# Three SBUF rings of an attention stage one buffer deeper, and a new set of planner ranks

## The chip, the cores and the metric

The kernel runs on one core of one Trainium2 chip. The metric is the device time of one execution in microseconds, and lower is better. Of the kernel before three timed runs are given, and one more execution that was taken with the profiler; all rows below come from that one.

## The reference, cut to what matters

Three stages, all in float32: linear attention with an exponential feature map, then two feed-forward layers, each on 2304 tokens of width 512 with a hidden width of 2048.

```python
def phi(x):                                   # q, k: (4, 8, 576, 64), w_phi: (64, 128)
    proj = np.einsum('bhsd,df->bhsf', x, w_phi)
    proj = proj - np.max(np.abs(proj), axis=-1, keepdims=True)
    return np.concatenate([np.exp(proj), np.exp(-proj)], axis=-1)
q_p, k_p = (phi(q), phi(k))
kv = np.einsum('bhsf,bhsd->bhfd', k_p, v);  z = np.sum(k_p, axis=2)
num = np.einsum('bhsf,bhfd->bhsd', q_p, kv)
den = np.einsum('bhsf,bhf->bhs', q_p, z)[..., None] + 1e-06
...
h = x @ w_in;   g = np.where(h > 0.0, h, np.exp(np.minimum(h, 0.0)) - 1.0);  x = g @ w_out
h = x @ w2_in;  g = h * np.clip(h + 3.0, 0.0, 6.0) / 6.0;                   out = g @ w2_out
```

## The kernel before, in words

**A planner writes the order.** Nearly every piece of work is a `Step` with an engine, an estimated duration, the steps that it comes after, the ring tokens that it takes and uses, and a rank. `in_order` plays the engines forward in time on those estimates. At each turn it takes, on each engine, the steps that could start within 0.3 us (`WINDOW`) of the soonest one and picks the one of lowest rank. The instructions of each engine are then issued in the order that comes out. On the chip an engine works through that order strictly and waits where an operand is late. A ring of n buffers is a limit in the planner and, through the tile's `bufs`, in the kernel: the (n+1)th writer waits for the last reader of the first buffer.

**Attention** is done in 8 units u, each two heads of two batches, 576 rows each. The sequence is cut into nine row blocks; a tile has a name such as k01: side k, blocks 0 to 3 ("0") or 4 to 7 ("1"), head 0 or 1; x8 is the ninth block of both sides. For each tile the steps are:

- PJ (PE, L439): projection of raw k or q by w_phi into PSUM; 18 blocks times two heads in a unit, and each float32 product is recorded as two instructions. It uses 64 rows of the array. In units 1 to 7 the steps are PJk0 (all k tiles), PJx8 and PJq0 (all q tiles).
- MX and SB (DVE, L449, L463): peak of the absolute value, then projection minus peak, written to SBUF tile `shk` (ring KB), `shq` (ring QB) or `sh`.
- EX (ACT, L472): the two exponentials of a k tile, `shk` to `kp` (ring KPB). KV (PE, L501, 128 rows): accumulation of kv and z from `kp` and v. ST (ACT, L510): kv to SBUF.
- QT (PE, L515, 64 rows): transposition of `shq`. QE (ACT, L532): exponentials of q, into `e`.
- NM (PE, L554, 128 rows): numerators and denominators, three steps in a unit. RT (DVE, L562, L563): reciprocal of the denominator, tile `dn`. RB (DVE, L567): the quotient, tile `nr` (ring NRB). XT (PE, L515): its transposition. XC (ACT, L583): copy to the x tile of the feed-forward layer.

The rank of such a step is `u * PERIOD` minus the length of the work that hangs on it, plus `BIAS`, looked up by name and unit (`KVk10@0`), by name (`KVk10`), or by kind (`KV`).

**The layers** have their PE order written out by hand (the list `order`); 8 groups g per layer. A group has seven products P1 to P7 for each of two block pairs (L841, one level of Strassen's scheme; in the first pair P6, P5 and P3 add to the bank that P1 opened, with a copy by ACT, `snap` L863, in between), two products H for the fifth block (L855), and products O (L908) that add to the output, which DVE adds up in x (`sums`, L924). The weights arrive as 64-bit floats and are made into pairs of float32 parts by ACT, DVE (L772, L778) and POOL (L766, L782, L788, L799, L808). Activation results are split by ACT (L886) and DVE (`gate_lo`, L889). The operands X of a layer are sums and differences of the blocks of x (`x_add`, L818, steps a...), split into a high part (L824, steps h...) and a low part (`x_lo`, L827, steps l...). The list `ON_POOL` says which of the a... and l... steps run on POOL instead of DVE: a10S40 is layer 1 (of 0, 1), block pair 0, operand S4, half 0. `SHIFT` adds to the rank of a single step.

Of the kernel before, what the change touches and what calls it, by code (L numbers as in the profile page):

```python
# [23 lines left out]
KB, QB, KPB, EB, NRB, MXB, WB, GB = 3, 6, 3, 4, 2, 6, 3, 2  # L24
PERIOD, PROJ, TURN = 21.5, 0.228, 0.13
BIAS = {
# [1281 lines left out]
```

## Time and profile before

| | before |
|---|---|
| median of three runs | 891.4 us (891.36 to 891.97) |
| profiled execution | 891.67 us |
| its span, first to last instruction | 889.8 us |
| PE busy | 879.9 us, 99% |
| DVE, ACT, POOL busy | 647.7, 567.3, 415.4 us |
| granted TensorE clock, mean | 1.000 |

The profiled execution takes 1.9 us more than its span and lies 0.27 us above the median. Busy shares are means over stages with different limits. The attention stage runs to about 150 us, the first layer to about 500 us, the second to the end. PE's busy time is no measure of how densely it works, since its instructions overlap and their ends are modelled; the distance from start to start tells more.

### The profile page before, as it was taken

To read this page: it belongs to the slowest core of one execution; us is meant where nothing else is said; L and a number is where in the kernel's file an instruction comes from. 1 tells how busy PE (TensorE), PEld (TensorE's weight loads), DVE (VectorE), ACT (ScalarE), POOL (GpSimd) and SP (SyncE) were. 2 spreads that over 40 slices of the span, in tenths; PEclk is the share of its full clock that TensorE was granted. 3 is DMA by queue.
4 is the path that set the end of the run, shared out by engine and by line. 5 is a ranking of instruction groups with operands and counts; after the bars stand their busy time and mean duration, and the time that the engine had idled before them with its cause. 6 is when DMAs were issued, how large, how long until landed. Compare 5 with 4: busy or idle time off the path is not lost.

```text
span 889.8 us, 18053 instructions
## 1 busy us (share of the span) xinstructions
PE 879.9 (99%) x7018; PEld 753.1 (85%) x7018; DVE 647.7 (73%) x1190; ACT 567.3 (64%) x1215; POOL 415.4 (47%) x584
## 2 busy tenths in 40 slices
PE   8999999999999999999999999999999999999998
PEld 7999997888888888888888788888888888888887
DVE  6999987647676767776777997576767676767656
ACT  6887889877575756565667777755545454545331
POOL 0268517745444444444444866565535354444200
PEclk9999999999999999999999999999999999999999
DMA  8545310011111111101111001112111111110013
GB/s 253 147 141 134 110 51 14 13 60 47 48 49 48 48 44 40 60 34 51 36 48 56 17 13 60 48 36 82 49 60 37 48 48 48 48 48 25 1 71 143
DMA packets 42678, 53.66 MB, mean 60 GB/s; under 512 B 21344, under 2 KB 21728, under 8 KB 42592
## 3 DMA queue, kind: packets, MB, share of 16 engines
q1 hardware_dynamic: 42448, 52.44, 18.8%
q8 instruction: 55, 0.90, 0.4%
q14 instruction: 31, 0.25, 0.1%
q10 hardware_dynamic: 144, 0.07, 0.0%
HBM read 47.78 MB, written 4.72 MB: 59 GB/s over the span
## 4 chain that ended last, share of the span: by engine, by line
PE 94%; DVE 5%; issue 0%; ACT 0%; DVEq 0%
PE ps_y L908 44%; PE ps_h L841 34%; PE ps_h L855 5%; PE ps_a L501 3%; PE ps_p L439 3%; PE ps_n L554 3%; PE ps_t L515 2%; DVE mx L449 1%; DVE shk L463 1%; DVE shq L463 1%; DVE nr L567 1%; PE ps_w L349 0%; DVE x L924 0%; DVE dn L563 0%; DVE dn L562 0%
## 5 line engine op out<-in xcount | busy, mean ns | idle before, releaser
L924 DVE TENSOR_TENSOR x<-ps_y,x 128x512 f32<-128x512 f32 (+1 forms) x267 | 174.9, 659 | 86.3 <-PE ps_y L908 82.9
L841 PE MATMUL ps_h<-x_S,w_in 128*128 128x512 f32 x768 | 190.2, 390 | 1.4 <-ACT mb L863 1.4
L841 PEld LDWEIGHTS ps_h<-x_S,w_in 128*128 128x128 f32 x768 | 143.7, 188 | 31.9 <-ACT mb L863 2.2
L841 PE MATMUL ps_h<-x_A,w_in 128*128 128x512 f32 x576 | 143.6, 390 | 0.0
L799 POOL TENSOR_TENSOR w_in<-w_bi,w_in 128x256 fp32r<-128x256 f32 x128 | 95.8, 766 | 70.4 <-ACT w_in L795 70.0
L841 PEld LDWEIGHTS ps_h<-x_A,w_in 128*128 128x128 f32 x576 | 107.2, 188 | 21.7
L908 PE MATMUL ps_y<-gb,w_out 128*128 128x512 f32 (+1 forms) x576 | 119.1, 354 | 0.8 <-DVE gb L889 0.5
L908 PE MATMUL ps_y<-w_out,gb 128*128 128x512 f32 (+1 forms) x486 | 117.5, 386 | 0.0
L908 PEld LDWEIGHTS ps_y<-gb,w_out 128*128 128x128 f32 x576 | 96.8, 189 | 17.5 <-DVE gb L889 1.0
L908 PEld LDWEIGHTS ps_y<-w_out,gb 128*128 128x128 f32 x486 | 90.6, 188 | 18.5
L766 POOL TENSOR_SCALAR w_a<-w_a 128x256 f32<-128x256 f32 x128 | 53.9, 422 | 98.3 <-ACT w_a L761 96.3
L782 POOL TENSOR_TENSOR w_bi<-w_bi,w_a 128x256 int32<-128x256 int32 x64 | 48.4, 758 | 108.7 <-DVE w_a L778 108.7
L908 PE MATMUL ps_y<-ga,w_out 128*128 128x512 f32 x384 | 92.6, 390 | 0.0
L908 PE MATMUL ps_y<-w_out,ga 128*128 128x512 f32 x384 | 92.3, 390 | 0.0
L908 PEld LDWEIGHTS ps_y<-w_out,ga 128*128 128x128 f32 x384 | 71.2, 188 | 14.2
L908 PEld LDWEIGHTS ps_y<-ga,w_out 128*128 128x128 f32 x384 | 71.2, 188 | 14.1
L782 POOL TENSOR_TENSOR w_bo<-w_bo,w_a 128x256 int32<-128x256 int32 x64 | 49.3, 772 | 65.3 <-DVE w_a L778 65.3
L882 DVE SCALAR_TENSOR_TENSOR ps_h<-ma,ps_h 128x512 f32<-128x512 f32 x80 | 55.4, 694 | 30.8 <-ACT ma L878 17.6
L863 ACT COPY mb<-ps_h 128x512 f32<-128x512 f32 x64 | 37.7, 589 | 58.0 <-PE ps_h L841 57.9
L808 POOL TENSOR_TENSOR w_out<-w_bo,w_out 128x256 fp32r<-128x256 f32 x64 | 47.3, 739 | 55.0 <-ACT w_out L804 54.5
L868 DVE TENSOR_TENSOR ps_h<-ps_h,mb 128x512 f32<-128x512 f32 x64 | 44.5, 696 | 35.9 <-ACT w_a L761 21.4
L889 DVE TENSOR_TENSOR gb<-ps_h,gb 128x512 fp32r<-128x512 f32 x80 | 54.5, 684 | 10.7 <-ACT gb L886 10.5
(80 smaller groups left out, 1455.8 us busy)
## 6 DMA issues: line engine op xcount, KB each, us to landing
w<-in_moe_w_in_dram SPq DMA_DIRECT2D x64, 256.0 KB, 2.6
w<-in_moe_w_out_dram SPq DMA_DIRECT2D x64, 256.0 KB, 2.6
vb<-in_v_dram SPq DMA_DIRECT2D x16, 288.0 KB, 4.9
out_dram<-x SPq DMA_DIRECT2D x17, 256.0 KB, 2.0
raw_k<-in_k_dram SPq DMA_DIRECT2D x7, 576.0 KB, 4.8
raw_q<-in_q_dram SPq DMA_DIRECT2D x7, 576.0 KB, 4.0
raw_k<-in_k_dram SPq DMA_DIRECT2D x1, 320.0 KB, 4.3
raw_q<-in_q_dram SPq DMA_DIRECT2D x1, 320.0 KB, 4.6
```

The lines of the kernel that those rows point to most:

```text
L766: nc.gpsimd.tensor_scalar(out=st["a"], in0=st["a"], scalar1=W_MOST, scalar2=W_LEAST, op0=ALU.min, op1=ALU.max)
L782: nc.gpsimd.tensor_tensor(out=b_, in0=b_, in1=st["a"].bitcast(I32), op=ALU.add)
L799: nc.gpsimd.tensor_tensor(out=t[:, 1], in0=F[key], in1=t[:, 0].bitcast(F32), op=ALU.subtract)
L808: nc.gpsimd.tensor_tensor(out=t[:, 1], in0=F.pop((m, w, 1, c)), in1=t[:, 0].bitcast(F32), op=ALU.subtract)
L841: nc.tensor.matmul(out=PS[ps_], lhsT=t[:, a_, kk], rhs=X[pr, op][x_][kk], start=(opens and i == 0), stop=(i == 5), skip_group_check=True,)
L855: nc.tensor.matmul(out=PS[ps_][:, 256 * fi:256 * fi + 256], lhsT=t[:, a_, kk], rhs=XB["x"][x_][2 * half + kk], start=(i == 0), stop=(i == ...
L863: nc.scalar.copy(out=MAIN[key], in_=PS[ps_])
L868: V.tensor_tensor(out=PS[to], in0=PS[ps_], in1=MAIN[key], op=ALU.add)
L882: V.scalar_tensor_tensor(out=PS[ps_], in0=MAIN[key], scalar=s, in1=PS[ps_], op0=o0, op1=o1)
L889: V.tensor_tensor(out=GG[key][:, 1], in0=PS.pop(ps_), in1=GG[key][:, 0].bitcast(F32), op=ALU.subtract)
L908: nc.tensor.matmul(out=o, lhsT=a_, rhs=b_, start=(fi + j == 0), stop=(fi == 1 and j == 2),)
L924: V.tensor_tensor(out=part, in0=ps, in1=part, op=ALU.add)
```

## The change

Three ring sizes rise by one: KB (the k tiles after the subtraction, `shk`) 3 to 4, KPB (their exponentials, `kp`) 3 to 4, NRB (the quotients, `nr`) 2 to 3. All of `BIAS`, most of `SHIFT`, and the list `ON_POOL` (34 names to 24: 18 taken out, 8 put in) are replaced. No instruction is added or removed; the order within each engine changes, and some of the a... and l... steps change engine.

```diff
 PB, TB = 6, 6
-KB, QB, KPB, EB, NRB, MXB, WB, GB = 3, 6, 3, 4, 2, 6, 3, 2
+KB, QB, KPB, EB, NRB, MXB, WB, GB = 4, 6, 4, 4, 3, 6, 3, 2
 PERIOD, PROJ, TURN = 21.5, 0.228, 0.13
 BIAS = {
-    "EX": -1284.5, "EXk00": -1287.9, "EXk00@0": -1229.4, "EXk00@7": -1290.5, "EXk01": -1250.5,
...
-    "EXx80@7": -1242.9, "KV": 1569.7, "KVk00": 688.3, "KVk00@0": 682.5, "KVk00@7": 808.9,
-    "KVk01": 633.4, "KVk01@0": 645.8, "KVk01@7": 620.8, "KVk10": 1610.3, "KVk10@7": 1634.4,
-    "KVk11": 1597.7, "KVk11@0": 1563.8, "KVx80": 1557.8, "KVx80@0": 1532.5, "KVx81": 1583.7,
-    "KVx81@0": 1549.4, "KVx81@7": 1541.4, "MX": -3939.8, "MXk00@7": -3937.8, "MXk01": -4172.3,
...
-    "MXx80@7": -3946.6, "MXx81": -4129.4, "MXx81@0": -4119.1, "MXx81@7": -4091.7, "NM": -92.1,
-    "NM0": -74.9, "NM1@7": -90.8, "NM2@0": -105.6, "NM2@7": -636.7, "PJ": 1001.6, "PJk0": 758.9,
-    "PJk0@0": 794.6, "PJk0@7": 747.3, "PJk1": 975.9, "PJk1@0": 520.4, "PJq0": 947.9,
-    "PJq0@0": 909.3, "PJq0@7": 856.1, "PJq1": 927.0, "PJq1@0": 399.3, "PJx8": 751.8,
...
+    "EX": 25.3, "EXk00": 26.5, "EXk00@7": 27.2, "EXk01": 78.0, "EXk01@0": 73.1, "EXk10": 49.5,
...
+    "EXx80": 59.2, "EXx80@7": 37.3, "KV": 378.3, "KVk00": 385.8, "KVk00@0": 349.3, "KVk00@7": 405.1,
+    "KVk01": 502.1, "KVk01@0": 510.3, "KVk01@7": 503.0, "KVk10": 675.9, "KVk10@0": 1437.7,
+    "KVk10@7": 687.0, "KVk11": 385.7, "KVk11@7": 461.5, "KVx80": 423.0, "KVx80@0": 418.8,
+    "KVx80@7": 312.8, "KVx81": 399.1, "KVx81@0": 456.9, "KVx81@7": 356.4, "MX": -6882.6,
...
+    "MXx81@7": -6951.9, "NM": -1437.3, "NM0": -1632.4, "NM0@7": -1579.5, "NM1@0": -1579.8,
+    "NM1@7": -1576.6, "NM2": -1468.9, "NM2@0": -1511.6, "NM2@7": -1471.5, "PJ": 4015.9,
+    "PJk0": 4028.6, "PJk0@0": 4003.2, "PJk0@7": 4039.1, "PJk1": 3924.7, "PJk1@0": 1417.4,
+    "PJq0": 4043.7, "PJq0@0": 4053.6, "PJq1": 3951.8, "PJq1@0": 1361.5, "PJx8": 3983.4,
...
 ON_POOL = """
-a01S11 a01S21 a01S31 a01S40 a10S10 a10S11 a11S11 a11S20 l00S40 l00S41 l01A121 l01A221 l01S10
-l01S11 l01S21 l01S30 l01S31 l01S40 l01S41 l04x1 l04x2 l04x3 l10A220 l10A221 l10S10 l10S11 l10S40
-l11A110 l11A121 l11A220 l11S30 l11S31 l11S41 l14x3
+a01S10 a01S11 a01S31 a10S10 a10S40 a11S10 a11S11 a11S31 l00S40 l00S41 l01A221 l01S11 l01S30
+l01S31 l04x2 l04x3 l10A220 l10A221 l10S11 l10S30 l10S31 l11A221 l14x1 l14x3
 """.split()
```

## Rows read from the trace of the kernel before

**Rows 1.** Page, part 1: engine, busy us, share, instructions.

```profile
PE 879.9 (99%) x7018; PEld 753.1 (85%) x7018; DVE 647.7 (73%) x1190; ACT 567.3 (64%) x1215; POOL 415.4 (47%) x584
```

**Rows 2.** Chain that ended last, whole run: start us, us, what, instructions.

```profile
53.75 4.61 PE ps_n L554 x144
...
240.88 5.44 PE ps_h L841 x24
...
287.52 5.44 PE ps_h L841 x24
```

**Rows 3.** The same chain, one unit of attention.

```profile
103.37 4.58 PE ps_n L554 x144
107.95 0.69 PE ps_t L515 x12
108.64 1.84 PE ps_p L439 x32
110.48 0.18 PE ps_t L515 x6
110.66 2.02 PE ps_a L501 x64
112.68 0.96 PE ps_t L515 x20
113.64 2.64 PE ps_a L501 x96
```

**Rows 4.** Groups of PE instructions over the run: KV and NM, with counts.

```profile
L501 PE MATMUL ps_a<-vb,kp 128*64 128x65 f32 (+1 forms) x1280 | 40.0, 224 | 1.3 <-ACT kp L472 0.7 <-issue 0.5
L554 PE MATMUL ps_n<-st,e 128*64 128x65 f32 x1152 | 36.7, 222 | 0.0
```

**Rows 5.** Busy time by window: start:end, length, PE, PEld, DVE, ACT, POOL, clock.

```profile
53.75:70.30 16.55, 16.34 (x438) 15.45 (x438) 15.71 (x34) 14.91 (x39) 11.84 (x15) 1.00 0.54 150
...
132.81:153.06 20.25, 18.90 (x229) 15.63 (x230) 13.82 (x26) 18.42 (x39) 13.49 (x13) 1.00 0.05 16
...
497.00:515.00 18.00, 17.23 (x88) 14.13 (x87) 17.25 (x28) 13.40 (x29) 16.01 (x16) 1.00 0.00 0
```

**Rows 6.** Timeline, the unit of rows 3: start, us, engine, what, [idle before].

```profile
105.24 2.19 ACT L472 ACTIVATE kp<-shk 128x512 f32<-128x512 f32 x4 [0.69 <-DVE shk L463]
...
107.49 0.68 DVE L463 TENSOR_TENSOR shk<-ps_p,mx 128x512 f32<-128x512 f32 x1
...
108.27 0.19 DVE L563 RECIPROCAL dn<-dn 128x6 f32<-128x6 f32 x1
...
108.57 0.56 DVE L567 TENSOR_TENSOR nr<-ps_n,dn 128x384 f32<-128x384 f32 x1
...
111.84 1.15 ACT L472 ACTIVATE kp<-shk 128x512 f32<-128x512 f32 x2 [0.61 <-ACT x L583]
...
113.56 2.07 ACT L532 ACTIVATE e<-ps_t 128x512 f32<-128x512 f32 x4 [0.56 <-PE ps_t L515]
```

**Rows 7.** Timeline of the first unit: PE's KV and QT with waits.

```profile
12.58 0.34 PE L501 MATMUL ps_a<-vb,kp 128*64 128x65 f32 x4 [0.49 <-ACT kp L472]
...
14.73 0.97 PE L515 MATMUL ps_t<-ident,shq 64*128 64x64 f32 x16 [0.60 <-DVE shq L463]
```

**Rows 8.** Chain at the start of the first layer: ACT's copies, then products H.

```profile
144.18 0.60 ACT mb L863
...
146.51 0.59 ACT mb L863
...
150.19 2.87 PE ps_h L855 x24
```

**Rows 9.** Timeline between the two layers: DVE, and PE waiting for it.

```profile
503.29 1.12 DVE L818 TENSOR_TENSOR x<-x 128x512 f32<-128x512 f32 x1
...
506.86 5.27 PE L908 MATMUL ps_y<-gb,w_out 128*128 128x512 f32 x22 [0.53 <-DVE gb L889]
...
509.34 0.67 DVE L818 TENSOR_TENSOR x<-x 128x512 f32<-128x512 f32 x1
```

152 rows, old and new, of tables (BIAS, SHIFT) are left out of this document.

## The prediction

> **What bounds the kernel now.** I read the page's busy line first: PE is busy for 99% of the span, DVE for 73% [rows 1]. No stretch shows PE at less than full clock, 2.4 GHz [rows 5]. A busy PE is not a dense PE, so the second view is the chain that ended last, where start-to-start distances count. In the first layer a group begins at 240.88 and the next at 287.52, 46.64 us later [rows 2]. A group holds 84 products P and 96 products O of 512 columns, 5.44 / 24 = 0.2267 us each [rows 2], 40.80 us, and 48 products of 256 columns (24 H, 24 O of the fifth block) at 2.87 / 24 = 0.1196 us [rows 8], 5.74 us. That is 46.54 of 46.64 us. So the layers are PE's own time, 16 such groups, some 740 us in which a rank can move nothing that counts. What can move is the attention stage, its two ends, and the passage between the layers.
>
> Third, one unit of attention. NM begins at 53.75 in one unit and at 103.37 three units later, a period of 16.54 us [rows 2, 3]. What PE must do in it: NM 144 instructions, 4.58 us; KV 160, of which 128 at 2.02 / 64, 4.04 us, and the ninth block's 32 at 2.64 - 2.02 = 0.62 us; PJ 72 at 1.84 / 32, 4.14 us; transpositions 54 at 0.18 / 6, 1.62 us [rows 3]; the counts of KV and NM are those of the run, 1280 and 1152, over 8 units [rows 4]. Sum 15.00 us. So 1.54 us of each period go on changes between 64 and 128 rows and on short waits, and PE is 91% dense. DVE is busy 15.71 of 16.55 us [rows 5]: it has 0.84 us left. Two engines are close to full, and neither is the sole bound.
>
> **The three buffers by themselves.** The question for each is whether its ring is the last thing that a writer waits for.
>
> `shk`: two tiles are read by ACT's four exponentials from 105.24 to 107.43; the third tile is written at 107.49 [rows 6]. With three buffers never more than two are live here, and the fourth buys nothing in this order: 0.
>
> `kp`: the fourth tile's exponentials begin at 111.84 after 0.61 us of idle ACT, which the row puts down to ACT itself [rows 6]. The real releaser is the ring. KV's 64 instructions begin at 110.66 and the first tile's half of them ends at 110.66 + 1.01 = 111.67 [rows 3], 0.17 us earlier. So this ring binds, once in the unit. What is it worth? The exponentials end at 112.99; that tile's KV is among the 96 instructions from 113.64, behind 0.62 us of the ninth block and a tile's 1.01 us, so some 2.3 us later. And ACT's next work waits 0.56 us for PE anyway [rows 6]. The cover is that slack: the buffer alone gives PE 0, and costs nothing.
>
> The Trainium skill (Perfetto Trace Analysis, Optimization Strategy) says that the same gap repeating on the engine that should be saturated can mean too few buffers. ACT shows such a gap; by that rule, were ACT the saturated engine, 0.61 us in seven units would make 4.3 us and a time near 887. ACT has a second gap right behind, so the row speaks against taking it.
>
> `nr`: the third quotient starts at 108.57, after its reciprocal, which runs from 108.27 to 108.46 [rows 6]. The transposition that frees the first buffer is in the first half of the twelve from 107.95 [rows 3]; even by a late count it ends at about 108.3. The reciprocal is last, so this buffer is worth 0 too.
>
> **The new order in the steady units.** What the deeper `kp` ring allows is another order on PE. Lower rank goes first. Before, the biases of the first two KV tiles were 621 to 809, those of projections (unit 0 apart) 711 to 1002, of the last KV tiles 1541 to 1634: KV falls into two pieces, with 20 transpositions between them. These take 0.96 us where 20 at 0.03 would be 0.60, so the split costs 0.36 us [rows 3]. After, unit 0 apart, all KV stand at 310 to 690 and the projections at 3980 to 4045, with room for four `kp` tiles. I expect KV in fewer pieces. No row shows that order. Its bounds: at best all of the 1.54 us but two changes of row count, each near the 0.33 us that the twelve transpositions behind NM take beyond 12 at 0.03 [rows 3], so 0.9 us a unit, 6.3 us in seven; at worst one more split a unit, 0.36, 2.5 us lost. I take one split saved, the row nearest to what the ranks say: 7 x 0.36 = **-2.5 us**. Where a unit's KV waits for its four exponentials instead, other PE work must be there to cover it; the projections are, as the last by rank.
>
> **The first unit.** PE waits 0.49 and 0.60 us for exponentials and subtractions [rows 7], 1.09 us together. Unit 0 has ranks of its own in the new set. Bounds: -1.1 and, for a like amount of new waits, +1.1. A third, **-0.4 us**, since DVE and ACT set these times and their work is the same.
>
> **Into the first layer.** Between P6, P5 and P3 PE waits for two copies by ACT, 0.60 and 0.59 us [rows 8]. That order is written by hand and stays; only attention's rest can fill the gaps. Seven preparing steps net move from POOL to DVE for this layer (eight leave the list, one enters); they belong to the second block pair and the fifth block, and DVE is busy 13.82 of 20.25 us there [rows 5], which is their cover: at 0.67 us each [rows 9] 4.7 us in 6.4 us of idle time, more behind it. **0**, bounds -1.2 and +1.3 us.
>
> **Between the layers.** DVE is busy 17.25 of 18 us, PE waits 0.53 us for `gate_lo` [rows 5, 9], and a little more shows as 17.23 busy of 18, 0.77 us in all. For the second layer's first pair as many steps leave POOL as enter; for its second pair seven leave and three enter, four more on DVE, 2.7 us at 0.67 [rows 9]. The second pair's products come behind a whole first pair, so I take **0**; bounds -0.8 (all waiting gone) and +2.7 us.
>
> The sum: 891.67 - 2.5 - 0.4 = 888.8 us for the profiled execution. That lies 0.27 us above the median of the runs, so **888.5 us** for the median.
>
> **The rivals.** *No difference (0.25).* PE's excess is changes of row count and the planner's own 0.3 us window, and the new order has as many of both; rings that do not bind give nothing. For it: the three readings of 0 above. Time 889.6 to 893, near 891.
>
> *Slower by late projections (0.10).* With PJ last of all on PE, the next unit's k tiles reach DVE later, and DVE becomes the sole bound. It has 0.84 us of slack a unit. A delay by one KV tile, 1.01 us, costs 0.17 us in seven units, 1.2 us; by two tiles, 2.02 us, it costs 1.18 a unit, 8.3 us. It decides from the point at which PJk0 starts more than 0.84 us later against the unit's NM than now. Midway +4.7: 896 us. Against it: a step is ranked only among those that can start, and a PJ that stands alone goes at once.
>
> *Slower between the layers (0.10).* The four extra DVE steps fall ahead of a `gate_lo` at 500 to 510 us: +2.7 us, 894 us. It decides if any of them gets ahead of PE's 506.86. One such sum took 1.12 us there against 0.67 us later [rows 9], so the price can be half as high again. The Trainium skill (SBUF — State Buffer, Who interferes with whom) says that a DVE instruction with two SBUF inputs contends with a GpSimd one that reads SBUF; the stretched row agrees, and by it steps taken off POOL also spare DVE collisions.
>
> *Much faster (0.07).* The best order of the steady units: 6.3 us there and 1.1 in the first unit, 884.0 us for the median. It needs DVE to keep up with a period of 15.6 us, against 15.71 busy now, which some of the weights' share would have to leave.
>
> **How the numbers follow.** A measurement of this kernel can tell about 0.2%, 1.8 us, from no change. My forecast, 885 to 889.6, has 0.48. With the much faster case, faster has 0.55; same 0.25; slower 0.20. The range from 884.5 to 893.8 leaves out part of the much faster case and the most of the two slower ones, under 0.2 in all.
>
> **What would show it.** Right: the distance between NM blocks falls from 16.54 to about 16.2 us; KV comes as one run of 160 or nearly so; the fourth tile's exponentials no longer begin 0.2 us after the first tile's KV ends; the layers' groups stay at 46.6 us. Wrong: the period is unchanged with as many pieces on PE, or DVE waits more for projections than now, or PE's waits between 497 and 515 us exceed 0.77 us. If the gain comes from there or from the start, the size may be right and the reason is not.

## The result and the profile after

The changed kernel takes 904.03 us (median of five runs, 902.45 to 905.95) against 891.4 us for the kernel before. The ratio is 1.0131, 95% interval 1.0117 to 1.0144: slower by some 11.7 us by the ratio. The forecast was 888.5 us with a range to 893.8. The profiled execution took 905.95 us, the longest of the five, and its span is 904.2 us.

The page's first line for the kernel after, against [rows 1]:

```profile
PE 883.7 (98%) x7018; PEld 755.3 (84%) x7018; DVE 648.4 (72%) x1200; ACT 567.8 (63%) x1215; POOL 402.9 (45%) x574
```

PE has the same instructions and is busy 3.8 us longer, and the span grew by 14.4 us, so most of the loss is PE standing idle. Ten steps moved from POOL (584 to 574) to DVE (1190 to 1200). The starts of NM place the loss; they come from the timeline of PE, in units 0, 1 and 7 (each unit's NM is longer than the pieces that are printed here).

```profile
24.40 4.69 PE L553 MATMUL ps_n<-st,e 128*64 128x65 f32 x144 [0.49 <-ACT st L509]
...
49.13 2.06 PE L553 MATMUL ps_n<-st,e 128*64 128x65 f32 x48
...
149.38 1.79 PE L553 MATMUL ps_n<-st,e 128*64 128x65 f32 x54
```

In the kernel before these three starts are 21.15, 37.12 and 135.70 us. From NM of unit 0 to NM of unit 1 it now takes 24.73 us instead of 15.97, 8.8 of the 14.4 us, and unit 0's NM itself comes 3.3 us later. The six units behind unit 1's NM take 100.25 us instead of 98.58. What comes after unit 7's NM takes 754.8 instead of 754.1 us. The layers hardly moved; the start is where the time went. PE's timeline there:

```profile
17.48 0.49 PE L438 MATMUL ps_p<-wphi,raw_k 64*128 64x128 f32 x4
17.80 0.39 PE L438 MATMUL ps_p<-wphi,raw_q 64*128 64x128 f32 x4
18.03 0.39 PE L438 MATMUL ps_p<-wphi,raw_k 64*128 64x128 f32 x4
18.25 0.39 PE L438 MATMUL ps_p<-wphi,raw_q 64*128 64x128 f32 x4
20.53 0.37 PE L514 MATMUL ps_t<-ident,sh 64*128 64x64 f32 x2 [1.89 <-DVE sh L462]
...
32.24 3.79 PE L500 MATMUL ps_a<-vb,kp 128*64 128x65 f32 x128
35.97 2.06 PE L438 MATMUL ps_p<-wphi,raw_q 64*128 64x128 f32 x32
...
40.09 0.97 PE L514 MATMUL ps_t<-ident,shq 64*128 64x64 f32 x16 [1.62 <-DVE shq L462]
...
44.48 1.20 PE L514 MATMUL ps_t<-ident,shq 64*128 64x64 f32 x16 [3.30 <-ACT w_in L794]
45.47 3.73 PE L438 MATMUL ps_p<-wphi,raw_k 64*128 64x128 f32 x32
```

Three things are to be seen. At 17.48 two steps PJx8 follow each other, those of unit 0 and of unit 1, and then PE waits 1.89 us for DVE's subtraction. From 32.24 on all of unit 1's remaining KV runs in one piece, and only then its q projections, at 35.97; the transpositions that need them wait 1.62 and 3.30 us. (The row puts the 3.30 us down to a weight step of ACT; the first of DVE's two subtractions into `shq` from 43.66 us on ends at about 44.3, and these transpositions read `shq`.) And the 32 projections at 45.47 take 3.73 us instead of 2.00. DVE's timeline of the same stretch gives the other side:

```profile
18.22 1.42 DVE L448 TENSOR_REDUCE mx<-ps_p 128x2 f32<-128x256 f32 x4 [2.28 <-PE ps_p L438]
19.56 0.49 DVE L771 SCALAR_TENSOR_TENSOR w_bi<-w,w_bi 128x256 int32<-128x256 int32 x1
19.97 0.41 DVE L462 TENSOR_TENSOR sh<-ps_p,mx 128x256 f32<-128x256 f32 x1
20.31 0.46 DVE L771 SCALAR_TENSOR_TENSOR w_bi<-w,w_bi 128x256 int32<-128x256 int32 x1
20.69 0.41 DVE L462 TENSOR_TENSOR sh<-ps_p,mx 128x256 f32<-128x256 f32 x1
...
34.39 0.42 DVE L771 SCALAR_TENSOR_TENSOR w_bi<-w,w_bi 128x256 int32<-128x256 int32 x1 [2.98 <-ACT w_bi L756]
...
38.05 1.29 DVE L448 TENSOR_REDUCE mx<-ps_p 128x4 f32<-128x512 f32 x2 [2.04 <-PE ps_p L438]
```

DVE takes four peaks of two units and weight work ahead of the subtractions that unit 0 waits for; later it is idle for 2.98 us, ended by a weight step, and for 2.04 us, ended by a projection: PE makes none between 23.3 and 35.97 us. The windows of the kernel after (columns as in rows 5) show the clock and the two passages:

```profile
40.00:45.00 5.00, 1.57 (x30) 1.35 (x30) 5.00 (x9) 3.63 (x11) 2.94 (x5) 0.83 0.65 225
45.00:50.00 5.00, 5.00 (x60) 4.78 (x58) 1.56 (x5) 3.69 (x9) 2.83 (x5) 0.50 0.01 3
...
155.00:185.00 30.00, 27.14 (x132) 21.63 (x132) 20.11 (x30) 25.12 (x50) 15.78 (x13) 1.00 0.00 1
505.00:525.00 20.00, 20.00 (x101) 16.76 (x100) 18.97 (x32) 16.53 (x33) 16.42 (x16) 1.00 0.07 21
```

From 45 to 50 us the granted clock is 0.50, the 1.2 GHz level, after PE had been busy for 1.57 of 5 us. Into the first layer PE is busy 27.14 of 30 us; among its waits is one of 1.51 us for `gate_lo` at 169 us, which the kernel before does not have. Between the layers, on the other hand, PE's 0.77 us of waiting [rows 5] are gone; everything stands 13.7 us later here, and PE is busy without a gap from 505 to 535 us.

### The profile page after: what moved, and what is told of

The parts are those of the page before. It is cut to its first block, busy times and chain, and to the rows that moved or that the text cites. A ratio compares the mean times of both kernels' runs of the same rounds, so it can differ in the third digit from the quotient of the medians.

```text
span 904.2 us, 18082 instructions
## 1 busy us (share of the span) xinstructions
PE 883.7 (98%) x7018; PEld 755.3 (84%) x7018; DVE 648.4 (72%) x1200; ACT 567.8 (63%) x1215; POOL 402.9 (45%) x574
## 4 chain that ended last, share of the span: by engine, by line
PE 91%; DVE 7%; issue 1%; ACT 1%; DVEq 0%; ACTq 0%
PE ps_y L907 43%; PE ps_h L840 34%; PE ps_h L854 5%; DVE mx L448 3%; PE ps_p L438 3%; PE ps_a L500 2%; DVE shk L462 1%; PE ps_t L514 1%; PE ps_n L553 1%; DVE shq L462 1%; DVE nr L566 1%; DVE dn L562 0%; PE ps_w L348 0%; ACT e L531 0%; DVE w_bi L771 0%
## 5 line engine op out<-in xcount | busy, mean ns | idle before, releaser
L907 PEld LDWEIGHTS ps_y<-ga,w_out 128*128 128x128 f32 x384 | 71.1, 188 | 16.4 <-DVE ga L888 2.3
L448 DVE TENSOR_REDUCE mx<-ps_p 128x4 f32<-128x512 f32 (+1 forms) x80 | 47.4, 629 | 22.6 <-PE ps_p L438 22.6
```

Source lines behind the costliest of these rows:

```text
L448: V.tensor_reduce(out=mx[:, :n], in_=P[j, h], axis=AX.X, op=ALU.max, apply_absolute_value=True)
L907: nc.tensor.matmul(out=o, lhsT=a_, rhs=b_, start=(fi + j == 0), stop=(fi == 1 and j == 2),)
```

## The experiments

Ratios are to runs of the kernel before on the same chip, with 95% intervals; a ratio of 1.001 is 0.9 us. Line numbers of a run can differ by one or two from those of before.

**One rank put back.** Which of the new numbers does it? In unit 0 the changed kernel runs KVk10 ahead of PJx8; before it was the other way round. In the new set their biases are 1437.7 and 1448.5, 10.8 apart.

```diff
-    "KVk01": 502.1, "KVk01@0": 510.3, "KVk01@7": 503.0, "KVk10": 675.9, "KVk10@0": 1437.7,
+    "KVk01": 502.1, "KVk01@0": 510.3, "KVk01@7": 503.0, "KVk10": 675.9, "KVk10@0": 1610.3,
```

> The changed kernel with one number put back: the bias of unit 0's third KV tile (KVk10) from 1437.7 to the 1610.3 that it had before, so that PE again does the first projection of the ninth block ahead of that KV. Theory A (one exchange of two PE steps in unit 0 lets weight work in ahead of attention, and the rest follows): nearly all of the loss goes; unit 1's NM begins near 37 us instead of 49.1, and the time is 887 to 891 us. Theory B (projections ranked behind all KV starve DVE, in unit 1 first): PJq0 still has a higher number than every KV, unit 1 stays late, 900 us or more. Theory C (the steps moved from POOL to DVE cost the time in the passages to the layers): no change from 904 us but for a us or two.

Measured: 891.54 us, ratio 0.9988 (0.9978 to 0.9997). One number takes the whole loss away, and a little more: theory A. NM of units 0, 1 and 7 in this run:

```profile
21.52 4.42 PE L553 MATMUL ps_n<-st,e 128*64 128x65 f32 x144
...
37.59 4.75 PE L553 MATMUL ps_n<-st,e 128*64 128x65 f32 x144
...
136.16 4.42 PE L553 MATMUL ps_n<-st,e 128*64 128x65 f32 x144
```

This run is the clean counterpart of the changed kernel, since only that number differs. Its span is 889.4 us, 14.8 less: 2.88 at unit 0's NM (24.40 - 21.52), 8.66 from there to unit 1's (24.73 - 16.07), 1.68 in the next six units (100.25 - 98.57), and 1.58 after unit 7's NM, of which the wait of PE for `gate_lo` at 169 us makes 1.51.

**The same exchange in the kernel before.**

```diff
-    "KVk01": 633.4, "KVk01@0": 645.8, "KVk01@7": 620.8, "KVk10": 1610.3, "KVk10@7": 1634.4,
+    "KVk01": 633.4, "KVk01@0": 645.8, "KVk01@7": 620.8, "KVk10": 1610.3, "KVk10@0": 700.0, "KVk10@7": 1634.4,
```

> The kernel before with one number added: the bias of unit 0's KVk10 at 700, below the 752 of the ninth block's projection, so that the same two PE steps change places; everything else as before, its rings and its projection ranks too. Theory A: the same kind of loss appears, 4 to 10 us, so 895 to 902 us, with unit 1's NM at 39 us or later instead of 37.2. Theory B: the projections keep their ranks, so at most 1 us, 891 to 892.5. Theory C: no change, 891.4 us.

Measured: 899.48 us, ratio 1.0076 (1.0056 to 1.0095), so 6.8 us lost by one exchange under the old ranks. NM of units 0 and 1 start at 23.51 and 42.70 us, 19.19 apart: between the 15.97 of before and the 24.73 of the changed kernel. The exchange hurts in either set, and more in the new one. DVE and PE in unit 0 of this run:

```profile
18.00 1.42 DVE L449 TENSOR_REDUCE mx<-ps_p 128x2 f32<-128x256 f32 x4 [2.29 <-PE ps_p L439]
19.33 1.40 DVE L463 TENSOR_TENSOR sh<-ps_p,mx 128x256 f32<-128x256 f32 x4
...
20.23 0.34 PE L515 MATMUL ps_t<-ident,sh 64*128 64x64 f32 x4 [1.83 <-DVE sh L463]
```

DVE again takes four peaks, here without weight work before the subtractions, and PE waits 1.83 us, against 1.89 in the changed kernel. So the late projection and the four peaks make that wait without any weight work.

**What the exchange does: DVE's order.** PE's pair stays exchanged; only unit 1's two peaks of the ninth block are held back on DVE.

```diff
 BIAS = {
+    "MXx80@1": 3000.0, "MXx81@1": 3000.0,
```

> The changed kernel, PE's exchanged pair of unit 0 left as it is, with the ranks of unit 1's two peaks of the ninth block (MXx80, MXx81) raised to 3000, so that DVE does not take them ahead of unit 0's subtractions of the ninth block. Theory A1 (the exchange hurts because it lets unit 1's ninth-block projection run directly behind unit 0's, and DVE, which ranks peaks first, then does four peaks, and weight work, before the two subtractions that unit 0 waits for): nearly all of the loss goes, unit 1's NM begins at 38 to 39.5 us, time 890 to 894 us. Theory A2 (PE's later projection of the ninth block costs by itself, whatever DVE does): unit 1's NM stays at 47 us or later and the time at 900 us or more.

Measured: 894.37 us, ratio 1.0023 (1.0013 to 1.0032): 9.6 of the 11.7 us are back (1.0131 - 1.0023 of 891.4). Unit 1's NM begins at 38.88 us, 16.07 behind unit 0's. DVE's timeline of this run:

```profile
18.09 0.76 DVE L449 TENSOR_REDUCE mx<-ps_p 128x2 f32<-128x256 f32 x2 [2.27 <-PE ps_p L439]
18.76 0.74 DVE L463 TENSOR_TENSOR sh<-ps_p,mx 128x256 f32<-128x256 f32 x2
19.42 0.49 DVE L772 SCALAR_TENSOR_TENSOR w_bi<-w,w_bi 128x256 int32<-128x256 int32 x1
```

DVE's wait of 2.27 us for the late projection is still there; what is gone is the pair of foreign peaks, and with it the weight work, between unit 0's peaks and its subtractions. Unit 0's NM begins at 22.81 us, some 1.3 later than with one rank put back: that much is left to PE's later projection by itself (theory A2 falls). DVE's order costs most of the loss (A1). Unit 1's q projections start at 28.10 us in this run, ahead of its KV again. In the kernel before KVk10 stands between the two PJx8 steps, and DVE has the time to subtract before the second one arrives.

**Unit 1: q projections behind KV.** Unit 0 stays as in the changed kernel; five KV steps of unit 1 are ranked behind that unit's PJq0.

```diff
 BIAS = {
+    "KVk01@1": 4060.0, "KVk10@1": 4060.0, "KVk11@1": 4060.0, "KVx80@1": 4060.0, "KVx81@1": 4060.0,
```

> The changed kernel, unit 0 left as it is, with the KV of unit 1 except its first tile ranked at 4060, behind that unit's q projection (PJq0, 4043.7). Theory D (in unit 1 PE does all six KV steps before PJq0, and DVE idles for want of projections): unit 1's NM moves from 49.1 to about 46 us, 2.5 to 4.5 us of the 12.6 come back, 899.5 to 901.5 us. If the idle DVE of unit 1 only follows from what unit 0 lost: no change, 903 to 905 us.

Measured: 898.26 us, ratio 1.0069 (1.0054 to 1.0084): 5.5 us back, more than the 2.5 to 4.5 expected. PE in units 0 and 1:

```profile
19.85 0.37 PE L515 MATMUL ps_t<-ident,sh 64*128 64x64 f32 x2 [1.89 <-DVE sh L463]
...
20.59 3.02 PE L439 MATMUL ps_p<-wphi,raw_k 64*128 64x128 f32 x32
...
30.61 1.15 PE L501 MATMUL ps_a<-vb,kp 128*64 128x65 f32 x32
31.69 0.40 PE L515 MATMUL ps_t<-ident,nr 64*128 64x64 f32 x6
31.93 2.00 PE L439 MATMUL ps_p<-wphi,raw_q 64*128 64x128 f32 x32
...
42.88 4.73 PE L554 MATMUL ps_n<-st,e 128*64 128x65 f32 x144
```

The q projections start at 31.93 instead of 35.97 us, NM 17.72 us behind unit 0's (25.16) instead of 24.73. So 7.0 of the 8.7 us that unit 1 lost come from that order. (By distances it is more than by the medians, since the profiled execution of the changed kernel lies 1.9 us above its median.) The part beyond the expectation may be the clock: the window 40 to 60 us shows 1.00 in this run, 0.83 in the changed kernel. But the clock fell in this run too, earlier: it is 0.66 in the window 20 to 25 us, where 32 projections take 3.02 us, behind a wait of 1.89 us that left it at 1.00 in the changed kernel.

**The clock.** Filler products where PE waits.

```diff
             for h in range(2):
                 row_pair(ps, 64 * h, SH["x8"][:, h, 1])
+            for _ in range(10 if u == 1 else 0):
+                nc.tensor.matmul(out=ps[0][:, 256:384], lhsT=blank, rhs=blank, start=True, stop=True)
```

> The changed kernel with ten more products of a blank tile (20 recorded instructions, about 2.1 us of PE at full clock) behind unit 1's transposition of the ninth block, into unused columns of its bank, where PE waits 3.3 us before the next transpositions. If the granted clock fell (0.83 of full in the window from 40 to 60 us) because PE stood idle there: the clock stays at 1.00 in that window, the 32 projections behind the wait take 1.85 instead of 3.5 us, and 1.5 to 2.5 us come back, 901.5 to 902.5 us. If the clock has another cause, or if the filler delays the exponentials of the ninth block: 904 us or more.

Measured: 902.79 us, ratio 1.0120 (1.0105 to 1.0135), an interval that overlaps that of the changed kernel; by the time alone it is open. The timeline says more:

```profile
40.25 4.13 PE L527 MATMUL ps_t<-blank 128*128 128x128 f32 x20
44.31 0.71 PE L514 MATMUL ps_t<-ident,shq 64*128 64x64 f32 x16
44.92 2.39 PE L438 MATMUL ps_p<-wphi,raw_k 64*128 64x128 f32 x32
```

The filler itself took 4.13 us instead of the 2.1 expected: the windows show the granted clock at 1.00 from 40.0 to 40.7 us and at 0.50 from there to 44.1, so it fell half a microsecond after the filler had begun, and my expectation that it would stay up was wrong. But it rose sooner: the 32 projections took 2.39 instead of 3.73 us, and NM of the two units lie 22.79 instead of 24.73 us apart. By these rows the low clock adds some 1.9 us in this place. That it follows from the waiting fits the means (0.994 to 0.996 in all five runs of the changed kernel, 1.000 in the ten with one rank put back), but it is not shown as a rule: a wait of 2.36 us at 37.6 us in the run with the same exchange in the kernel before left the clock at 1.00, and in the kernel before with the deeper rings, below, it was 0.50 from 16.4 to 19.8 us, where no wait of PE in the ten microseconds ahead was longer than 0.6 us.

**The rings, under the old ranks and the new.** Three runs: the kernel before with the deeper rings, the changed kernel with the old ones, and the kernel with one rank put back with the old ones.

```diff
-KB, QB, KPB, EB, NRB, MXB, WB, GB = 3, 6, 3, 4, 2, 6, 3, 2
+KB, QB, KPB, EB, NRB, MXB, WB, GB = 4, 6, 4, 4, 3, 6, 3, 2
```

> The kernel before with the three rings one deeper (KB 4, KPB 4, NRB 3) and its own ranks. My reading that the shk and nr rings never bind and that the kp ring's wait is covered: 891.0 to 892.0 us, no difference. If the rings were what slows the changed kernel: 895 us or more. If the covered wait of the kp ring were on the path: 887 us.

Measured: 893.25 us, ratio 1.0010 (0.9998 to 1.0022): no difference that can be told from none. ACT's wait of 0.60 us ahead of a fourth tile's exponentials, which stands in units 1, 4, 5 and 6 of the kernel before, is in none of these units here.

> The changed kernel with the rings as before (KB 3, KPB 3, NRB 2) and the new ranks. Theories A, B and C alike put the loss on ranks: 902 to 906 us, as the changed kernel. If the deeper rings cause the loss: about 891 us. If they are worth something under these ranks: slower than 906 us.

Measured: 906.51 us, ratio 1.0159 (1.0144 to 1.0174): the loss is in the ranks. The interval only touches that of the changed kernel; if the difference of 2.5 us is real, the deeper rings help here too.

> The changed kernel with unit 0's KVk10 put back to 1610.3 (as in the run with one rank restored, 891.5 us) and the rings as before (KB 3, KPB 3, NRB 2). If the deeper kp ring is worth nothing under the new ranks either: 891 to 892 us. If the new order needs four kp tiles: 893.5 to 897 us, with a longer distance between two NM blocks in one or more of the units 3 to 5.

Measured: 895.76 us, ratio 1.0039 (1.0024 to 1.0054), against 0.9988 with the deeper rings: here the rings are worth 4.5 us. NM of units 4 and 5 in this run, on PE, and ACT in between:

```profile
88.04 4.56 PE L553 MATMUL ps_n<-st,e 128*64 128x65 f32 x144
...
97.09 1.15 ACT L471 ACTIVATE kp<-shk 128x512 f32<-128x512 f32 x2 [0.63 <-ACT x L582]
...
101.13 0.68 PE L500 MATMUL ps_a<-vb,kp 128*64 128x65 f32 x15 [0.84 <-issue]
...
105.89 4.42 PE L553 MATMUL ps_n<-st,e 128*64 128x65 f32 x144
```

This unit takes 17.85 us, against 16.24 with the deeper rings (86.84 to 103.08), and the wait of ACT that I had read in rows 6 is there again. But it does not make the unit long: the next unit has the same wait, 0.63 us at 114.59, and takes 16.10 us. PE's own wait in the long unit is 0.84 us in the middle of KV, and another of 0.94 us stands at 50.60, in unit 1, which takes 17.30 us. For neither does the profile name a releaser ("issue"), and with the deeper rings PE has no such wait. How the rings lead to it is open, and which of the three it is was not run apart.

**The moved steps alone.** The new `SHIFT` and `ON_POOL` in the kernel before, 10 steps net from POOL to DVE.

```diff
-a01S11 a01S21 a01S31 a01S40 a10S10 a10S11 a11S11 a11S20 l00S40 l00S41 l01A121 l01A221 l01S10
...
+a01S10 a01S11 a01S31 a10S10 a10S40 a11S10 a11S11 a11S31 l00S40 l00S41 l01A221 l01S11 l01S30
...
```

> The kernel before (its rings and its BIAS) with the new SHIFT and the new ON_POOL alone: ten steps net moved from POOL to DVE, the attention ranks untouched. Theory C (these moves cost time in the passages to the layers, four DVE steps ahead of PE between 497 and 515 us): 893 to 895 us, with PE waiting more than 0.77 us there. If they are harmless, and it is they that took PE's wait between the layers away in the changed kernel: 0.3 to 1.0 us less than before in the same rounds, PE busy 18.0 of 18.0 us in that window.

Measured: 892.04 us, ratio 0.9993 (0.9984 to 1.0003): no loss, so theory C falls, and a gain that can't be told from none. The window between the layers shows PE without a wait and DVE full, so it is the moved steps that took PE's 0.77 us there away:

```profile
497.00:515.00 18.00, 18.00 (x92) 15.15 (x91) 17.98 (x29) 14.70 (x30) 16.79 (x16) 1.00 0.00 0
```

## Why the prediction was wrong

**What bounds the kernel:** right. What comes after unit 7's NM took 0.7 us longer, and the passage between the layers changed by less than a microsecond.

**The three buffers by themselves:** right, as far as it was run. 0 was said for each; together they measured 1.0010, with 1 inside the interval. That the ring makes ACT's gap is borne out, since the gap goes with the deeper rings; but it stands in four of the units 1 to 6 and not in every one. And the value held for the order of the kernel before only. Under the new ranks with one put back the same rings are worth 4.5 us, so 0 was a property of an order, not of a ring. The Trainium skill (Perfetto Trace Analysis, Optimization Strategy) reads a repeated gap as a possible want of buffers where the engine is the one that should be saturated. ACT is not that engine, and here its gap went and the time stayed.

**The steady units, -2.5 us:** wrong in its mechanism. I expected KV in fewer pieces, since KV now ranks ahead of PJ. What splits KV, by the ranks and the rows, is not PJ but QT, which ranks ahead of both in both sets (about -2800 before, -2950 after): with one rank put back the 20 transpositions still stand between two pieces of KV. No run changed QT's rank. The run with one rank put back has the new steady order without the accident at the start, and its six units take 98.57 us, those of before 98.58, in one execution each. The term was 0 by these rows, and everything but the one rank measured -1.1 us (0.9988) where -2.9 was forecast.

**The first unit, -0.4 us:** wrong, and this is the step that decided. I gave unit 0 two lines, bounded by the waits that PE had there, plus or minus 1.1 us. Against the run with one rank put back it lost 2.9 us itself and set off 8.7 in unit 1. Two errors are in it. I bounded a reorder by the size of present waits, while what it can cost is set by what other engines pull forward when one of them waits. And I read the ranks by kind ("unit 0 apart") and left out the one unit whose own numbers decide: `KVk10@0` at 1437.7 stands in the quoted diff beside the numbers that I used.

**Into the first layer, 0:** wrong by 1.5 us. The wait for `gate_lo` at 169 us lies outside the bound of +1.3. It came with the exchange and not with the steps moved to DVE: the runs with one rank put back and with the held peaks have those steps and not this wait.

**The cover that I named for KV:** "other PE work must be there; the projections are, as the last by rank". In unit 1 KV did run in one piece, 160 instructions with six transpositions between, just as I had hoped for the steady units; and the projections were what DVE lacked. The work that I counted as filler was the next engine's input.

**The rival of late projections (0.10):** close in its mechanism and wrong in its place. I had PJk0 in every unit at 896 us; it was PJq0, in one unit, which starts 11.57 us behind unit 0's NM (35.97 - 24.40). Five KV steps put behind it brought 5.5 us back. My point against it, that a PJ which stands alone goes at once, fits the steady units, which kept their period; that it is the reason was not tested.

**The rival between the layers (0.10) and the term 0 there:** the term was right, the rival did not happen, and the moved steps alone measure 0.9993.

**What is settled and what is open.** Shown by runs: one exchange of two steps in unit 0 is what separates 904 from 891.5 us, 12.7 us by the ratios (1.0131 - 0.9988). It works through DVE's order (holding two peaks back returns 9.6 us) and, in unit 1, through PE doing KV before PJq0 (5.5 us). The two overlap, since holding back DVE's peaks also keeps unit 1's order from going wrong. The low clock adds about 2 us by the distances, which the times alone don't confirm. The span with the held peaks stays 3.0 us above that with one rank put back: 1.3 of it stand before unit 0's NM (22.81 against 21.52), and 1.7 in the six units behind unit 1's, which take 100.26 us, as in the changed kernel, and not 98.57. In the changed kernel and with the held peaks PE waits about a microsecond in the middle of unit 4's KV (1.04 us at 111.77 and 1.09 at 101.58), for nothing that the profile names; with one rank put back it does not. Open: what that wait is. The weight work at 19.56 and 20.31 us was not tried apart, but under the old ranks PE's wait was 1.83 us without it, against 1.89. The kernel with one rank put back has the lowest ratio of all, 0.12% (0.03 to 0.22%) below the kernel before; the interval of the moved steps alone overlaps its own.

## What to carry to other kernels

In an order that a planner writes from ranks, cost a change of ranks at its ends first: in this kernel a wait in the unit in which the pipeline fills was not hidden, and the engine that waited there took up work of lower urgency, which then stood ahead of what the others needed. Before counting an engine's late work as cover, ask who consumes it: projections ranked last are free for PE and are the input of DVE. And rings that cost nothing under one order (1.0010) were worth 4.5 us under another, so a ring is read again with each order.

## What the runs showed of the hardware

The granted clock fell to the 1.2 GHz level in the middle of a kernel that holds 2.4 GHz otherwise: 0.50 from 45 to 50 us, after PE had been busy 1.57 of the 5 us before, and it was back at 0.99 from 50 to 55 us. It fell at about 43.3 us, within PE's wait of 3.30 us. With filler products from 40.25 us on it fell at about 40.7 us and was back sooner, as the windows of that run show:

```profile
40.00:44.00 4.00, 4.00 (x31) 3.93 (x26) 3.95 (x10) 2.07 (x4) 2.13 (x3) 0.59 0.72 245
44.00:48.00 4.00, 3.64 (x55) 3.10 (x53) 0.66 (x2) 3.58 (x12) 2.43 (x4) 0.98 0.02 4
```

So filling a wait late did not keep the clock up; it was back at about 44.2 us instead of 50.1. The length of a wait alone does not tell when the clock falls: behind the same wait of 1.89 us at the same point of the order it stayed at 1.00 in the changed kernel and fell to 0.50 in the run with unit 1's q projections ahead of KV.
